# Reading the moving operand of every float32r product as two runs in turn

## The chip, the cores and the metric

The kernel runs on one core of a Trainium2 chip, as one program and one launch. The metric is the device time of that program in microseconds, taken as the median of several runs. TensorE (PE in the profile) does the products, VectorE (DVE), ScalarE (ACT) and GpSimd (POOL) do the elementwise work, and SyncE (SP) issues the DMAs.

## The reference

An attention over a window of 128 positions feeds two feed-forward layers. What is computed, cut to what matters:

```python
# 4 batches, 8 heads, 576 positions, 64 per head -> x is 2304 tokens x 512
x = attention(q, k, v)                  # window 128, bias -slope*|i-j|, softmax
h = x @ moe_w_in                        # first layer: 512 -> 2048
x = (relu(h) ** 2) @ moe_w_out          # 2048 -> 512
gate = 1 / (1 + exp(-(x @ w_gate)))     # second layer: 512 -> 1536, twice
val = x @ w_val
out = (gate * val) @ w_out              # 1536 -> 512
```

The inputs are float32; the weights reach the chip as 64-bit floats and are turned into 32-bit ones by a few bit operations.

## The kernel before

**Products in three parts.** Outside the attention every product is made of float32r matmuls. An operand is split into a high part (an ACT copy that rounds to float32r) and a low part (operand minus high part, on DVE or POOL), and high x high, high x low and low x high are added up in PSUM. So each product of 128 x 128 weights with 256 or 320 columns is three matmuls. Each matmul loads its own 128-column stationary operand (PEld in the profile) and then streams its moving operand of 256 or 320 columns past it.

**Stage A.** The attention and the first layer run chunk by chunk. There are eight chunks of tokens; the first four have 256 columns, the last four 320. For each of 16 slices of the hidden width, `h_step` makes h (lines 833 to 835, moving operand `x`), ACT takes Relu (847), DVE or ACT squares, an ACT copy through the helper at line 338 and a subtraction through the helper at line 335 write the two parts into the tile `gs` (850, 851), and `y_step` multiplies them with the output weights (870, moving operand `gs`). The products stand in the order H(f), Y(f-1), H(f+1), Y(f), so that a slice's elementwise work runs under the products of its neighbours. After the last slice `evac` copies the four y banks to SBUF, and they go to a scratch tensor in DRAM, 512 rows by tokens. The attention's own products and transposes are plain float32 and stand between these on TensorE.

**Weights of the second layer.** `prepare` turns them into 32 bits, splits them and their four Strassen sums into high and low parts (`split`, called by `pieces`), and `put` stores these in a scratch tensor. Each tile there holds high and low part of 256 columns side by side. `fetch` brings them back, one 256 KB tile at a time, for each block of tokens.

**Stage B.** The first block has 256 tokens (`xb` with n = 0, `gv`, `o_step`), and the other four have 512 each and go through Strassen's seven products (`xb`, `part`, `gv_strassen` at line 995, `o_strassen` at line 1168, `o_last` at line 1254). In the gate and value products the tokens are the moving operand; in the output products the weights are.

**What sets the order.** A planner (`Plan.schedule`) runs at build time. It gives each operation an engine, a place on it and a buffer, by priorities and assumed durations, and its list is written out as it stands. The change leaves those durations alone.

Of the kernel before, what the change touches and what calls it, by code (L numbers as in the profile page):

```python
# [287 lines left out]
def attention_moe_moe2_kernel(ctx: ExitStack, tc, q, k, v, w_in, w_out1, w_gate, w_val, w_out2, out):  # L288
# [54 lines left out]

    def chunk_steps(n):
        l = [("H", n, 0)]
        for f in range(1, F1):
            l += [("H", n, f), ("Y", n, f - 1)]
        return l + [("Y", n, F1 - 1)]
# [135 lines left out]
    def prepare(kind, f0, prio):  # L484
# [16 lines left out]
        as_halves = lambda p, z: p().rearrange("p k (z n) -> p z k n", z=2)[:, z]  # L501

        def pieces(t_, keys, k, prio):
            p = new("pp", [128, 2, 512], F32R)
            split(lambda: t_().rearrange("p (k n) -> p k n", k=2), lambda: as_halves(p, 0), lambda: as_halves(p, 1), keys, p, prio)
            put(u, p, k, prio + .1)
# [317 lines left out]
    def h_step(n, f, e0):  # L824
        N = width[n]
        w, x = W["in", f], X[n]
        ps = new("h", [128, 512], F32)
        xk = [(x, a, hp, p) for a in range(2) for hp in range(HP) for p in range(len(chunks[n]))]
        for half in range(2):
            def go(e, half=half):  # L830
                for cc in range(half * CC // 2, (half + 1) * CC // 2):
                    c = slice(cc * 128, cc * 128 + 128)
                    nc.tensor.matmul(ps()[:, :N], w[0]()[:, c], x()[:, 0, cc, :N], start=cc == 0, stop=False)  # L833
                    nc.tensor.matmul(ps()[:, :N], w[0]()[:, c], x()[:, 1, cc, :N], start=False, stop=False)  # L834
                    nc.tensor.matmul(ps()[:, :N], w[1]()[:, c], x()[:, 0, cc, :N], start=False, stop=cc == CC - 1)  # L835
# [13 lines left out]
        op({"ACT": act_ns(N)} if n >= 7 else {"DVE": dve_ns(N), "ACT": act_ns(N)}, square, r=[ps, g], w=[g], prio=ep)  # L849
        op({"ACT": act_ns(N)}, copy(lambda: gs()[:, 0, :N], lambda: g()[:, :N]), r=[g], w=[(gs, 0)], prio=ep)  # L850
        op(dve_or_pool(N), minus(lambda: gs()[:, 1, :N], lambda: g()[:, :N], lambda: gs()[:, 0, :N]),
           r=[g, (gs, 0)], w=[(gs, 1)], prio=ep, port=True)
        G[n, f] = gs
# [3 lines left out]
    def y_step(n, f, e0):  # L857
# [5 lines left out]
        for e_ in range(CC):  # L863
            y = Y[n][e_]

            def go(e, y=y, e_=e_):
                c = slice(e_ * 128, e_ * 128 + 128)
                for p, (a, b) in enumerate(((0, 0), (0, 1), (1, 0))):

                    nc.tensor.matmul(y()[:, c0:c0 + N], w[a]()[:, c], gs()[:, b, :N], start=f == 0 and p == 0 and n != 1,  # L870
# [4 lines left out]
        if f == F1 - 1:  # L875
            for e_ in range(CC):
# [3 lines left out]
                def evac(e, y=y, ys=ys):  # L880
                    if e == "ACT":
                        nc.scalar.activation(out=ys()[:, :N], in_=y()[:, c0:c0 + N], func=AF.Copy)
                    else:
                        nc.vector.tensor_copy(ys()[:, :N], y()[:, c0:c0 + N])
# [17 lines left out]
    def xb(n, prio):  # L902
        t0, NB = blocks[n]
        if n == 0:
            x = new("x", [128, 2, CC, NMAX], F32R)
            for c0 in range(0, CC, 2):
                ysg = new("ysg", [128, 512], F32)
                src = lambda ysg=ysg: ysg().rearrange("p (c t) -> p c t", c=2)
                part = lambda z, c0=c0: x()[:, z, c0:c0 + 2, :NB]
# [4 lines left out]
                op({"ACT": act_ns(512)}, copy(lambda part=part: part(0), src), r=[ysg], w=[(x, 0, c0)], prio=prio)  # L914
                op(dve_or_pool(512), minus(lambda part=part: part(1), src, lambda part=part: part(0)),
# [26 lines left out]
        def part(name, src, pr):  # L942
            (bh, ih), (bl, il) = where[name]
            op({"ACT": act_ns(512)}, copy(lambda: bh()[:, ih], flat(src)), r=[src], w=[(bh, ih)], prio=pr)
            op({"DVE": dve_ns(512)}, minus(lambda: bl()[:, il], flat(src), lambda: bh()[:, ih]), r=[src, (bh, ih)], w=[(bl, il)], prio=pr, port=True)
# [31 lines left out]
    def gv_strassen(n, kind, f, e0):  # L977
# [9 lines left out]
        def product(name, ps, start=False):  # L987
# [102 lines left out]
    def gv(n, f, e0):  # L1090
# [3 lines left out]
        for z, kind in enumerate(("gate", "val")):  # L1094
# [6 lines left out]
            def go(e, ps=ps, part=part):  # L1101
                for cc in range(CC):
                    nc.tensor.matmul(ps()[:, :NB], part(0, cc), x(0, cc), start=cc == 0, stop=False)
                    nc.tensor.matmul(ps()[:, :NB], part(0, cc), x(1, cc), start=False, stop=False)  # L1104
                    nc.tensor.matmul(ps()[:, :NB], part(1, cc), x(0, cc), start=False, stop=cc == CC - 1)
# [14 lines left out]
    def o_step(n, f, e0):  # L1120
# [4 lines left out]
        for t in range(NB // 128):  # L1125
            o = O[n][t]

            def go(e, t=t, o=o):
                c = slice(t * 128, t * 128 + 128)
                for k in range(2):  # L1130
                    for i, (a_, z) in enumerate(((ah, 0), (ah, 1), (al, 0))):
                        nc.tensor.matmul(o()[:, k * 256:k * 256 + 256], a_()[:, c], w[k]()[:, z * 256:z * 256 + 256],  # L1132
# [20 lines left out]
    def o_strassen(n, f, part, e0, last=False):  # L1153
# [82 lines left out]
    def o_last(n, f, part, e0):  # L1236
# [8 lines left out]
        for z, (i, j, ps, sum_, fresh) in enumerate(todo):  # L1245
            fine = (i, j) == (0, 1)
            for t in range(2):
                for part_ in range(2):
# [3 lines left out]
                    def go(e, t=t, part_=part_, hi=hi, lo=lo, ch=ch, wt=wt, ps=ps, fresh=fresh):  # L1252
                        for k, (a_, y) in enumerate(((hi, 0), (hi, 1), (lo, 0))):
                            nc.tensor.matmul(ps()[:, 256 * t:256 * t + 256], a_()[:, ch + 128 * t:ch + 128 * t + 128], wt()[:, 256 * y:256 * y + 256],
# [122 lines left out]
```

## Time and profile before

| | us |
|---|---|
| median of 3 runs | 959.66 (958.83 to 960.71) |
| span of the profiled execution, first to last instruction | 955.4 |
| TensorE busy, of that span | 941.8 |
| TensorE loading weights | 908.9 |
| VectorE busy | 630.4 |
| ScalarE busy | 559.8 |
| GpSimd busy | 186.4 |

The span is one execution under the profiler; the runs were timed without it. The 4.3 us between the span and the median lie outside the first and the last instruction. Busy times of the engines overlap. A matmul's duration in the trace includes the time in which its result drains, so the matmuls of a stream overlap each other; what one costs in a stream is read from start to start.

### The profile page before, as it was taken

The numbers are of one execution on the slowest core, as the hardware profiler recorded it, in microseconds if no ns is written. First come the engines' busy times: TensorE is split into PE (matmuls) and PEld (weight loads), VectorE is DVE, ScalarE is ACT, GpSimd is POOL, SyncE is SP. The second block draws the span as 40 slices with busy tenths as digits, with TensorE's granted clock in tenths as the row PEclk, the third lists the DMA queues.
The fourth block names the chain that finished last, engine by engine and source line by source line (L and its number), as shares of the span: only waits on it lengthen the run. The fifth ranks groups of instructions, "written<-read, shape, count | busy, mean of one in ns | idle before, by whom it ended". The sixth has DMA issues, their size and how long they took to land.

```text
span 955.4 us, 21188 instructions
## 1 busy us (share of the span) xinstructions
PE 941.8 (99%) x7656; PEld 908.9 (95%) x7656; DVE 630.4 (66%) x1621; ACT 559.8 (59%) x1496; POOL 186.4 (20%) x270
## 2 busy tenths in 40 slices
PE   8899999999999999999999999999999999999998
PEld 6689999999999999999999999999999999999998
DVE  7999988677676676767753234555855585476555
ACT  6987876777676586667554523544544544454442
POOL 3611111313132121123000010102312230122000
PEclk9999999999999999999999999999999999999999
DMA  9755547584665766665699791666877787678931
GB/s 230 178 166 169 170 128 227 203 228 154 188 182 175 215 191 173 193 187 177 223 300 385 286 322 43 210 212 211 264 236 219 226 268 223 212 240 277 331 100 45
DMA packets 181448, 199.83 MB, mean 209 GB/s; under 512 B 80097, under 2 KB 113377, under 8 KB 181345
## 3 DMA queue, kind: packets, MB, share of 16 engines
q1 hardware_dynamic: 181344, 198.48, 67.1%
q8 instruction: 61, 1.00, 0.5%
q14 instruction: 43, 0.34, 0.1%
HBM read 151.26 MB, written 47.19 MB: 208 GB/s over the span
## 4 chain that ended last, share of the span: by engine, by line
PE 94%; DVE 3%; ACT 1%; DMA 1%; SPq 1%; issue 0%; DVEq 0%
PE y L870 22%; PE pa L995 14%; PE pd L995 11%; PE o L1168 10%; PE h L833 7%; PE h L834 7%; PE h L835 7%; PE tv L806 3%; PE ts L679 2%; PE o L1132 2%; PE pd L1168 2%; PE tp L761 1%; DMA nq<-in_q_dram 1%; ACT st L711 1%; PE ts L670 1%; PE pv L1104 1%
## 5 line engine op out<-in xcount | busy, mean ns | idle before, releaser
L870 PE MATMUL y<-gs,wh 128*128 128x256 f32 (+1 forms) x1024 | 214.3, 301 | 1.3 <-DVE gs L335 1.3
L870 PEld LDWEIGHTS y<-gs,wh 128*128 128x128 f32 x1024 | 163.4, 189 | 8.5 <-issue 3.8
L833 PE MATMUL h<-x,wh 128*128 128x256 f32 (+1 forms) x512 | 154.2, 301 | 0.0
L834 PE MATMUL h<-x,wh 128*128 128x256 f32 (+1 forms) x512 | 151.3, 295 | 0.5 <-DVE x L335 0.5
L870 PE MATMUL y<-gs,wl 128*128 128x256 f32 (+1 forms) x512 | 151.4, 296 | 0.3 <-DVE wl L335 0.3
L835 PE MATMUL h<-x,wl 128*128 128x256 f32 (+1 forms) x512 | 151.2, 295 | 0.0
L338 ACT ACTIVATE cg<-pa 128x256 f32<-128x256 f32 x144 | 54.7, 382 | 109.6 <-PE pa L995 106.2
L847 ACT ACTIVATE r<-h 128x256 f32<-128x256 f32 (+1 forms) x128 | 51.9, 407 | 86.9 <-PE h L835 86.7
L335 DVE TENSOR_TENSOR gs<-r,gs 128x256 fp32r<-128x256 f32 (+1 forms) x122 | 58.0, 476 | 64.7 <-ACT gs L338 64.4
L833 PEld LDWEIGHTS h<-x,wh 128*128 128x128 f32 x512 | 96.7, 189 | 2.6 <-issue 1.0
L834 PEld LDWEIGHTS h<-x,wh 128*128 128x128 f32 x512 | 96.8, 189 | 0.7 <-DVE x L335 0.7
L870 PEld LDWEIGHTS y<-gs,wl 128*128 128x128 f32 x512 | 96.6, 189 | 0.5 <-DVE wl L335 0.5
L835 PEld LDWEIGHTS h<-x,wl 128*128 128x128 f32 x512 | 96.5, 189 | 0.0
L771 POOL TENSOR_SCALAR_AFFINE_SELECT pt<-pt 128x256 f32<-128x256 f32 (+1 forms) x120 | 61.5, 539 | 135.3 <-ACT pt L765 134.3
L995 PE MATMUL pa<-x,st 128*128 128x256 f32 x576 | 84.3, 282 | 0.0
L1011 DVE TENSOR_TENSOR cg<-cg,pd 128x256 f32<-128x256 f32 x96 | 40.4, 421 | 61.6 <-PE pd L995 60.3
L995 PEld LDWEIGHTS pa<-x,st 128*128 128x128 f32 x576 | 75.2, 189 | 0.0
L1168 PE MATMUL o<-wr,ah 128*128 128x256 f32 x414 | 68.0, 281 | 0.0
L711 ACT ACTIVATE st<-st,sm 128x128 f32<-128x128 f32 x144 | 56.6, 402 | 16.9 <-DVE sm L704 16.7
L1168 PE MATMUL o<-so,ah 128*128 128x256 f32 x414 | 64.0, 281 | 0.0
L338 ACT ACTIVATE gs<-r 128x256 fp32r<-128x256 f32 (+1 forms) x128 | 56.5, 442 | 6.2 <-PE y L870 3.3
L1168 PEld LDWEIGHTS o<-wr,ah 128*128 128x128 f32 x414 | 57.3, 189 | 0.0
(197 smaller groups left out, 2044.5 us busy)
## 6 DMA issues: line engine op xcount, KB each, us to landing
st<-wscr SPq DMA_DIRECT2D x192, 256.0 KB, 3.6
wscr<-pp SPq DMA_DIRECT2D x72, 512.0 KB, 3.4
so<-wscr SPq DMA_DIRECT2D x93, 256.0 KB, 4.1
raw<-in_moe_w_out_dram SPq DMA_DIRECT2D x28, 512.0 KB, 3.8
wr<-wscr SPq DMA_DIRECT2D x54, 256.0 KB, 5.3
raw<-in_moe_w_in_dram SPq DMA_DIRECT2D x16, 512.0 KB, 4.3
vs<-in_v_dram SPq DMA_DIRECT2D x24, 256.0 KB, 5.5
raw<-in_moe_w_gate_dram SPq DMA_DIRECT2D x12, 512.0 KB, 3.9
```

The costliest lines, as they stand in the source:

```text
L335: return lambda e: eng(e).tensor_tensor(out=out(), in0=a(), in1=b(), op=ALU.subtract)
L338: return lambda e: nc.scalar.activation(out=out(), in_=in_(), func=AF.Copy, scale=scale)
L711: op({"ACT": 386}, lambda e, x=x: nc.scalar.activation(out=st()[:, x, :], in_=st()[:, x, :], func=AF.Exp, bias=sm()[:, x:x + 1], scale=-1. ...
L771: op({"POOL": pool_sel(512 // nq)}, lambda e: nc.gpsimd.affine_select(out=pt_of(what, j), in_=pt_of("own", j), pattern=[[0, 512 // (nq * c ...
L833: nc.tensor.matmul(ps()[:, :N], w[0]()[:, c], x()[:, 0, cc, :N], start=cc == 0, stop=False)
L834: nc.tensor.matmul(ps()[:, :N], w[0]()[:, c], x()[:, 1, cc, :N], start=False, stop=False)
L835: nc.tensor.matmul(ps()[:, :N], w[1]()[:, c], x()[:, 0, cc, :N], start=False, stop=cc == CC - 1)
L847: op({"ACT": act_ns(N, True)}, lambda e: nc.scalar.activation(out=g()[:, :N], in_=ps()[:, :N], func=AF.Relu), r=[ps], w=[g], prio=ep, also ...
L870: nc.tensor.matmul(y()[:, c0:c0 + N], w[a]()[:, c], gs()[:, b, :N], start=f == 0 and p == 0 and n != 1, stop=f == F1 - 1 and p == 2, skip_ ...
L995: nc.tensor.matmul(ps()[:, :256], w()[:, z * 256 + cc * 128:z * 256 + cc * 128 + 128], x, start=start and cc == 0 and i == 0, stop=cc == 1 ...
L1011: op({"DVE": dve_ns(256)} if psum else dve_or_pool(256), lambda e: eng(e).tensor_tensor(out=quarter(i, j)(), in0=quarter(i, j)(), in1=src( ...
L1168: nc.tensor.matmul(o()[:, 256 * t:256 * t + 256], a_()[:, c_ + 128 * t:c_ + 128 * t + 128], w()[:, 256 * z:256 * z + 256], start=start and ...
```

## The change

A new helper, `in_turn`, takes a run of N columns as two halves of N/2 and reads them in turn: column 0 of the first half, column 0 of the second, column 1 of the first, and so on. In the built program the moving operand of a 256-column product was one run of 256 elements and is now 128 pairs, the two elements of a pair lying 128 elements (512 bytes) apart; with 320 columns they lie 160 elements apart. All 6,534 float32r products of the computation get this pattern: 4,998 of 256 columns and 1,536 of 320. The attention's float32 products, the transposes and the 50 spin products at the start keep theirs.

So that results come out in place, the order in which operands lie is changed where they are split. In the first layer `x` lies as before, so that h comes out with its columns in turn; the splits into `gs` read every second column of it (`from_turns`) and write two runs (`runs`), which puts the columns back in order, and the evacuation of y does the same. In the second layer the splits read every second element of the source and write the two halves of a run, so that reading in turn gives the original order. That holds for the weights of the output product (`pieces`), for the first block (`xb`) and for the Strassen operands (`part`).

No instruction is added or removed. Apart from line numbers, the rows of instructions on each of the five engines, with their buffers, are the same word for word before and after; only access patterns differ.

```diff
+    def in_turn(x):
+        return x.rearrange("p (i c) -> p c i", i=2)
+
+    def runs(x):
+        return x.rearrange("p (i c) -> p i c", i=2)
+
+    def from_turns(x):
+        return x.rearrange("p (c i) -> p i c", i=2)
...
-        as_halves = lambda p, z: p().rearrange("p k (z n) -> p z k n", z=2)[:, z]
+        if kind == "out2":
+            as_halves = lambda p, z: p().rearrange("p k (z i n) -> p z k i n", z=2, i=2)[:, z]
+            as_read = lambda t_: t_().rearrange("p (k n i) -> p k i n", k=2, i=2)
+        else:
+            as_halves = lambda p, z: p().rearrange("p k (z n) -> p z k n", z=2)[:, z]
+            as_read = lambda t_: t_().rearrange("p (k n) -> p k n", k=2)
...
-            split(lambda: t_().rearrange("p (k n) -> p k n", k=2), lambda: as_halves(p, 0), lambda: as_halves(p, 1), keys, p, prio)
+            split(lambda: as_read(t_), lambda: as_halves(p, 0), lambda: as_halves(p, 1), keys, p, prio)
...
-                    nc.tensor.matmul(ps()[:, :N], w[0]()[:, c], x()[:, 0, cc, :N], start=cc == 0, stop=False)
+                    nc.tensor.matmul(ps()[:, :N], w[0]()[:, c], in_turn(x()[:, 0, cc, :N]), start=cc == 0, stop=False)
...
-        op({"ACT": act_ns(N)}, copy(lambda: gs()[:, 0, :N], lambda: g()[:, :N]), r=[g], w=[(gs, 0)], prio=ep)
-        op(dve_or_pool(N), minus(lambda: gs()[:, 1, :N], lambda: g()[:, :N], lambda: gs()[:, 0, :N]),
+        op({"ACT": act_ns(N)}, copy(lambda: runs(gs()[:, 0, :N]), lambda: from_turns(g()[:, :N])), r=[g], w=[(gs, 0)], prio=ep)
+        op(dve_or_pool(N), minus(lambda: runs(gs()[:, 1, :N]), lambda: from_turns(g()[:, :N]), lambda: runs(gs()[:, 0, :N])),
...
-                    nc.tensor.matmul(y()[:, c0:c0 + N], w[a]()[:, c], gs()[:, b, :N], start=f == 0 and p == 0 and n != 1,
+                    nc.tensor.matmul(y()[:, c0:c0 + N], w[a]()[:, c], in_turn(gs()[:, b, :N]), start=f == 0 and p == 0 and n != 1,
...
-                        nc.scalar.activation(out=ys()[:, :N], in_=y()[:, c0:c0 + N], func=AF.Copy)
+                        nc.scalar.activation(out=runs(ys()[:, :N]), in_=from_turns(y()[:, c0:c0 + N]), func=AF.Copy)
                     else:
-                        nc.vector.tensor_copy(ys()[:, :N], y()[:, c0:c0 + N])
+                        nc.vector.tensor_copy(runs(ys()[:, :N]), from_turns(y()[:, c0:c0 + N]))
...
-            op({"ACT": act_ns(512)}, copy(lambda: bh()[:, ih], flat(src)), r=[src], w=[(bh, ih)], prio=pr)
-            op({"DVE": dve_ns(512)}, minus(lambda: bl()[:, il], flat(src), lambda: bh()[:, ih]), r=[src, (bh, ih)], w=[(bl, il)], prio=pr, port=True)
+            turns = lambda: src().rearrange("p c (t i) -> p c i t", i=2)
+            hi, lo = ((lambda b=b, k=k: b()[:, k].rearrange("p (c i t) -> p c i t", c=2, i=2)) for b, k in ((bh, ih), (bl, il)))
+            op({"ACT": act_ns(512)}, copy(hi, turns), r=[src], w=[(bh, ih)], prio=pr)
+            op({"DVE": dve_ns(512)}, minus(lo, turns, hi), r=[src, (bh, ih)], w=[(bl, il)], prio=pr, port=True)
...
-                        nc.tensor.matmul(ps()[:, :256], w()[:, z * 256 + cc * 128:z * 256 + cc * 128 + 128], x,
+                        nc.tensor.matmul(ps()[:, :256], w()[:, z * 256 + cc * 128:z * 256 + cc * 128 + 128], in_turn(x),
...
-                nc.tensor.matmul(o()[:, 256 * t:256 * t + 256], a_()[:, c_ + 128 * t:c_ + 128 * t + 128], w()[:, 256 * z:256 * z + 256],
+                nc.tensor.matmul(o()[:, 256 * t:256 * t + 256], a_()[:, c_ + 128 * t:c_ + 128 * t + 128], in_turn(w()[:, 256 * z:256 * z + 256]),
```

Left out are the same edits of the other matmul calls (lines 834, 835, 1103 to 1105, 1132, 1254) and of the split in `xb` for the first block.

## Rows read from the trace of the kernel before

**Rows 1.** The page: busy us (share of the span) and instructions of each engine

```profile
PE 941.8 (99%) x7656; PEld 908.9 (95%) x7656; DVE 630.4 (66%) x1621; ACT 559.8 (59%) x1496; POOL 186.4 (20%) x270
```

**Rows 2.** The page: the chain that ended last, share of the span by engine

```profile
PE 94%; DVE 3%; ACT 1%; DMA 1%; SPq 1%; issue 0%; DVEq 0%
```

**Rows 3.** TensorE's waits, longest and shortest: us in total, times, longest

```profile
PE warm L1332 <- DVE identr L382: 1.8, 1, 1.8
...
PE pa L995 <- DVE cg L1040: 0.2, 1, 0.2
```

**Rows 4.** Windows: us; each engine's busy us (instructions); PEclk granted; DMA share, GB/s

```profile
100.00:200.00 100.00, 100.00 (x852) 95.76 (x852) 82.69 (x205) 71.40 (x189) 18.00 (x28) 1.00 0.60 188
...
700.00:800.00 100.00, 100.00 (x845) 100.00 (x844) 60.80 (x122) 47.56 (x111) 20.83 (x18) 1.00 0.76 236
```

**Rows 5.** Groups on PE by shape: busy us, mean ns of one

```profile
L870 PE MATMUL y<-gs,wh 128*128 128x320 f32 x512 | 117.4, 316 | 0.0
L870 PE MATMUL y<-gs,wh 128*128 128x256 f32 x512 | 96.9, 286 | 1.3 <-DVE gs L335 1.3
...
L1254 PE MATMUL pa<-so,ah 128*128 128x256 f32 x6 | 1.0, 279 | 0.0
```

**Rows 6.** Timeline of PE in stage B: start us, us until the last has drained

```profile
699.74 0.88 PE L995 MATMUL pa<-x,st 128*128 128x256 f32 x6
700.46 0.88 PE L995 MATMUL pd<-x,st 128*128 128x256 f32 x6
701.18 0.51 PE L1168 MATMUL o<-so,ah 128*128 128x256 f32 x3
701.53 0.88 PE L995 MATMUL pa<-xp,wr 128*128 128x256 f32 x6
```

**Rows 7.** Timeline of PE late in stage A, 320 columns

```profile
506.00 0.31 PE L833 MATMUL h<-x,wh 128*128 128x320 f32 x1
...
507.76 0.46 PE L870 MATMUL y<-gs,wh 128*128 128x320 f32 x2
...
511.28 0.46 PE L870 MATMUL y<-gs,wh 128*128 128x320 f32 x2
```

**Rows 8.** Timeline of PE: float32 transposes of 128 columns, one group behind another

```profile
22.55 0.60 PE L580 MATMUL tk<-identr,nk 128*128 128x128 f32 x4
22.98 0.60 PE L761 MATMUL tp<-identr,st 128*128 128x128 f32 x4
```

**Rows 9.** Timeline of PE: the first products of the program (float32r spin products)

```profile
1.78 4.40 PE L1332 MATMUL warm<-identr 128*128 128x256 f32 x21 [1.78 <-DVE identr L382]
6.13 0.66 PE L580 MATMUL tq<-identr,nq 128*128 128x128 f32 x4
```

**Rows 10.** Groups on ACT: a read of every second word, and a contiguous one

```profile
L338 ACT ACTIVATE pp<-tw 128x512 fp32r<-128x512 f32 x36 | 22.5, 624 | 4.1 <-DVE tw L471 1.7 <-DMA wscr<-pp 1.5 <-DVE tg L471 0.6
...
L461 ACT ACTIVATE tw<-raw 128x512 f32<-128x512 f32 x18 | 12.0, 669 | 0.1
```

**Rows 11.** Groups on DVE: a contiguous subtraction, and one source of every second word

```profile
L335 DVE TENSOR_TENSOR pp<-tw,pp 128x512 fp32r<-128x512 f32 x33 | 24.0, 726 | 11.2 <-ACT pp L338 10.5
...
L471 DVE SCALAR_TENSOR_TENSOR tw<-raw,tw 128x512 int32<-128x512 int32 x18 | 13.0, 724 | 0.2
```

**Rows 12.** A group on POOL: a contiguous subtraction

```profile
L335 POOL TENSOR_TENSOR pp<-tg,pp 128x512 fp32r<-128x512 f32 x6 | 7.7, 1288 | 39.5 <-DVE ts L692 19.0 <-DVE gs L335 11.5 <-ACT pp L338 8.1
```

**Rows 13.** Evacuations of y, on ACT and on DVE

```profile
L882 ACT ACTIVATE yz<-y 128x320 f32<-128x320 f32 x8 | 3.5, 438 | 4.3 <-PE y L870 3.2 <-PE h L834 1.1
...
L884 DVE COPY yz<-y 128x320 f32<-128x320 f32 x8 | 3.8, 490 | 2.5 <-PE h L834 1.7 <-PE h L835 0.7 <-PE y L870 0.2
```

**Rows 14.** Timeline of ACT and of DVE around rows 7: the splits of one slice

```profile
507.96 0.44 ACT L847 ACTIVATE r<-h 128x320 f32<-128x320 f32 x1 [2.07 <-PE h L835]
...
509.44 0.49 DVE L335 TENSOR_TENSOR gs<-r,gs 128x320 fp32r<-128x320 f32 x1 [3.02 <-ACT gs L338]
```

More of the change, by code (lines that the diff above doesn't have):

```diff
@@ L832, in go @@
                     c = slice(cc * 128, cc * 128 + 128)
-                    nc.tensor.matmul(ps()[:, :N], w[0]()[:, c], x()[:, 0, cc, :N], start=cc == 0, stop=False)
-                    nc.tensor.matmul(ps()[:, :N], w[0]()[:, c], x()[:, 1, cc, :N], start=False, stop=False)
-                    nc.tensor.matmul(ps()[:, :N], w[1]()[:, c], x()[:, 0, cc, :N], start=False, stop=cc == CC - 1)
+                    nc.tensor.matmul(ps()[:, :N], w[0]()[:, c], in_turn(x()[:, 0, cc, :N]), start=cc == 0, stop=False)
+                    nc.tensor.matmul(ps()[:, :N], w[0]()[:, c], in_turn(x()[:, 1, cc, :N]), start=False, stop=False)
+                    nc.tensor.matmul(ps()[:, :N], w[1]()[:, c], in_turn(x()[:, 0, cc, :N]), start=False, stop=cc == CC - 1)
             op({"PE": 3 * CC // 2 * pe_ns(N)}, go, r=xk + list(w), w=[ps] + ([("late",)] if n == NC - 1 and f == F1 - 2 else []), prio=e0 + half * .1)
@@ L908, in xb @@
                 src = lambda ysg=ysg: ysg().rearrange("p (c t) -> p c t", c=2)
-                part = lambda z, c0=c0: x()[:, z, c0:c0 + 2, :NB]
+                turns = lambda ysg=ysg: ysg().rearrange("p (c t i) -> p c i t", c=2, i=2)
+                part = lambda z, c0=c0: x()[:, z, c0:c0 + 2, :NB].rearrange("p c (i t) -> p c i t", i=2)
                 op({"SP": 475}, lambda e, c0=c0, src=src: nc.sync.dma_start(
@@ L913, in xb @@
                    prio=prio - 6, data=728, also=[x])
-                op({"ACT": act_ns(512)}, copy(lambda part=part: part(0), src), r=[ysg], w=[(x, 0, c0)], prio=prio)
-                op(dve_or_pool(512), minus(lambda part=part: part(1), src, lambda part=part: part(0)),
+                op({"ACT": act_ns(512)}, copy(lambda part=part: part(0), turns), r=[ysg], w=[(x, 0, c0)], prio=prio)
+                op(dve_or_pool(512), minus(lambda part=part: part(1), turns, lambda part=part: part(0)),
                    r=[ysg, (x, 0, c0)], w=[(x, 1, c0)], prio=prio)
@@ L1102, in go @@
                 for cc in range(CC):
-                    nc.tensor.matmul(ps()[:, :NB], part(0, cc), x(0, cc), start=cc == 0, stop=False)
-                    nc.tensor.matmul(ps()[:, :NB], part(0, cc), x(1, cc), start=False, stop=False)
-                    nc.tensor.matmul(ps()[:, :NB], part(1, cc), x(0, cc), start=False, stop=cc == CC - 1)
+                    nc.tensor.matmul(ps()[:, :NB], part(0, cc), in_turn(x(0, cc)), start=cc == 0, stop=False)
+                    nc.tensor.matmul(ps()[:, :NB], part(0, cc), in_turn(x(1, cc)), start=False, stop=False)
+                    nc.tensor.matmul(ps()[:, :NB], part(1, cc), in_turn(x(0, cc)), start=False, stop=cc == CC - 1)
             op({"PE": 3 * CC * pe_ns(NB)}, go, r=xkeys + w + [("late",)], w=[ps], prio=e0 + z)
@@ L1131, in go @@
                     for i, (a_, z) in enumerate(((ah, 0), (ah, 1), (al, 0))):
-                        nc.tensor.matmul(o()[:, k * 256:k * 256 + 256], a_()[:, c], w[k]()[:, z * 256:z * 256 + 256],
+                        nc.tensor.matmul(o()[:, k * 256:k * 256 + 256], a_()[:, c], in_turn(w[k]()[:, z * 256:z * 256 + 256]),
                                          start=f == 0 and k == 0 and i == 0, stop=f == F2 - 1 and i == 2, skip_group_check=True)
@@ L1253, in go @@
                         for k, (a_, y) in enumerate(((hi, 0), (hi, 1), (lo, 0))):
-                            nc.tensor.matmul(ps()[:, 256 * t:256 * t + 256], a_()[:, ch + 128 * t:ch + 128 * t + 128], wt()[:, 256 * y:256 * y + 256],
+                            nc.tensor.matmul(ps()[:, 256 * t:256 * t + 256], a_()[:, ch + 128 * t:ch + 128 * t + 128], in_turn(wt()[:, 256 * y:256 * y + 256]),
                                              start=fresh and t == 0 and part_ == 0 and k == 0, stop=part_ == 1 and k == 2, skip_group_check=True)
```

## The prediction

> **What bounds the kernel now.** I read the page first. TensorE is busy for 941.8 of 955.4 us [rows 1], and the chain that ended last runs through it for 94% of the span [rows 2]. Its list of waits has eleven rows, of which the longest is 1.8 us and the shortest 0.2 [rows 3]; all eleven add up to about 10 us, nearly all of it before 50 us. In the windows it is busy 100.00 of 100 us in the dense part of stage A and in stage B [rows 4]. So the end is set by the rate at which matmuls follow each other, and by little else.
>
> That rate is read from the timeline, start to start. In stage B, 15 products of 256 columns take 701.53 - 699.74 = 1.79 us, 119.3 ns each [rows 6], and the window from 700 to 800 us has 845 of them, 118.3 ns each [rows 4]. Late in stage A twelve of 320 columns take 507.76 - 506.00 = 1.76 us, 146.7 ns each [rows 7]. The granted clock is 1.00 there [rows 4], the upper of the two levels, 2.4 GHz, at which 256 columns stream in 106.7 ns and 320 in 133.3 ns. So each product costs 11.6 to 12.6 ns and 13.4 ns more than its columns. I call this the surplus. Two things are to be seen in it:
> - It hardly grows with the columns (12 against 13 ns), so it comes once per matmul, and each matmul has one load of 128 weight columns running beneath the stream of the one before.
> - It is gone where the moving operand is read at half the rate. Four float32 transposes of 128 columns, each with its own load, take 22.98 - 22.55 = 0.43 us, 108 ns each [rows 8], which is 0.83 ns per column; 128 columns at 1.2 GHz are 106.7 ns. The 21 spin products at the start take 6.13 - 1.78 = 4.35 us, 207 ns each [rows 9], where 256 columns at 1.2 GHz would be 213.
>
> So the load alone doesn't make the surplus. It appears when the moving operand is read at full rate while weights are read. That points to the reading of operands from SBUF, and the order of that reading is all that the change alters on TensorE.
>
> **The change part by part.** No instruction moves, so no queue is passed and no wait is added.
>
> *The products.* 6,534 get the new pattern. The list by shape has 33 rows of 256 columns, with 4,998 instructions, and five of 320 columns, with 1,536 (the first of each and the last stand in [rows 5]). The trace of before has no float32r product that hops, so I bound the new cost from both sides. Below: the surplus goes, and what stays is what the transposes keep, 108 - 106.7, about 2 ns with the rounding of the timeline [rows 8]. That saves 10 ns of 118.3 and 11 ns of 146.7: 4,998 x 10 = 50 us and 1,536 x 11 = 17 us, together 67 us. Above: each hop costs a read, and the moving operand comes at one column per cycle of the lower level [rows 9]: 207 ns for 256 columns and 207 x 320 / 256 = 259 ns for 320. That adds 4,998 x 89 = 445 us and 1,536 x 112 = 172 us, 617 us in all. I take the lower end. The transposes differ from the stream in type and shape as well, but the spin products are the same float32r product [rows 9], and in both the surplus is gone with the reading rate. So the surplus sits in the reading, and the reading is what is changed. That it changes for the better is an inference; no row shows it.
>
> *The splits.* They now read every second word. On ACT such a read of 512 took 669 ns where a contiguous one took 624 [rows 10], 45 ns more. About 102 splits of 512 columns and 128 of 256 or 320 (some 25 ns each by the same ratio) make 102 x 45 + 128 x 25 = 8 us on an engine that is busy for 559.8 of 955.4 us [rows 1]. On DVE an operation with one source of every second word took 724 ns, a contiguous subtraction 726 [rows 11], so nothing. POOL has no such row. A contiguous split there takes 1,288 ns [rows 12]; between nothing and a doubling I take nothing, as DVE shows. All this is hidden: a slice's h ends at 507.76, its splits end at 509.44 + 0.49 = 509.93, and its y products start at 511.28 [rows 7, 14], 1.35 us later. An added 25 ns disappears in that. Without this cover each of the 128 slices would pay it, 3 us.
>
> *The evacuations.* They read every second word of PSUM, for which there is no row: 32 of some 440 to 490 ns [rows 13], shared by ACT and DVE, two each per chunk. Between nothing and a doubling (0.9 us at each of seven changes of chunk, 6 us) I take nothing, because two slices of h stand between the last y of one chunk and the first of the next.
>
> *What is late next.* If products get faster, the work beside them must keep up. From 100 to 200 us DVE is busy for 82.7 of 100 us and ACT for 71.4 [rows 4]; were all 852 instructions there products of 256 columns, they would give up 8.5 us, and DVE would stand at 82.7 / 91.5 = 90%. Late in stage A the path from one slice to its use shortens by 24 x 11 = 0.26 us, and the 1.35 us of slack becomes 1.1. In stage B DVE is at 61% and the DMA engines at 0.76 [rows 4], which would become 66% and 0.83. So nothing takes over as the bound, but the planner's order has tight places in stage A. I let 6 us come back as new waits. At worst stage A, with 1,536 products of either width (15 + 17 us), gains nothing.
>
> *The sum.* 955.4 - 67 + 6 = 894 us of span. The median stands 4.3 us above the profiled span, so I predict **899 us**. With stage A gaining nothing it is 955.4 - 35 + 4.3 = 925; with no give-back 893; with two thirds of the surplus removed, 955.4 - 45 + 6 + 4.3 = 921. Its own range is 890 to 935.
>
> [...]
>
> **The rivals.**
>
> *The hop costs* (the other side). Neighbouring columns of the stream now lie 512 or 640 bytes apart, so a read may bring one column where it brought several, and TensorE can't be fed at 256 columns in 118.3 ns. For it: nothing in the trace reads a float32r moving operand in any order but straight through, and the transposes and spin products show what half the rate looks like. Against it: each of the two runs is still read in order, so whoever reads two runs side by side needs no more from memory than before. It decides from the point where a 256-column product takes more than 118.3 ns. In full it gives 955.4 + 617 + 4.3 = 1,577 us; a twentieth of its price gives 955.4 + 31 + 4.3 = 991.
>
> *The order of reading doesn't matter.* The surplus belongs to the hand-over from one set of weights to the next and is paid at full rate whatever the order. For it: it is the same for 256 and 320 columns, as a fixed hand-over would be. Against it: the transposes hand over weights too and keep only 2 ns. Then only the splits and evacuations count: 959.7 plus 0 to 6 us, 960 to 966. This is also the case in which the change doesn't do what it says, though the built program does carry the 128 pairs.
>
> *Something else takes over.* Products get faster, but the slices of stage A wait for DVE: 925 us as above. This is inside the forecast's own range.
>
> **How the numbers follow.** A measurement of this kernel can tell some 0.2%, 2 us, from no change. I give the forecast, with the third rival in it, 0.67; the order not mattering 0.13; the hop costing 0.20, of which a quarter pays so little that it stays below 990 us. The second splits about evenly between within 0.2% and slower by more. So faster 0.67, same 0.07, slower 0.26. The range must leave out no more than 2 in 10: from 890 it has to pass the second rival's 966 and the mild form of the first, so it ends at 990; left out are the full price of the hop (0.15) and a little below 890. The forecast's own range, 890 to 935, holds some 0.6 of the chance.
>
> **What would show it.** In the timeline of after, six products of 256 columns in stage B should start 0.65 us apart instead of 0.72, and twelve of 320 columns 1.63 instead of 1.76; the window from 700 to 800 us should hold some 920 products. The weight loads should follow in step. ACT's splits of 512 columns should read about 670 ns, DVE's stay near 726. TensorE's waits may grow from 10 to about 16 us, and those added should name DVE or ACT in stage A. The prediction is wrong in its main step if six products still take 0.72 us (the hand-over) or more (the hop), and wrong in its give-back if they are faster but the windows show TensorE below 97% anywhere between 60 and 900 us.

## The result and the profile after

The change takes the kernel from 959.5 to 916.9 us (913.7 to 918.6 in four runs). The ratio is 0.955, with a 95% interval of 0.953 to 0.958: 43 us, or 4.5%, faster. The forecast was 899 us. The profiled execution has a span of 911.5 us and is the quickest of the four; each of them lists a span 2.1 to 2.2 us below its time. The later executions of the kernel before, whose spans are listed too, show the same 2.1 to 2.2 us. So the 4.3 us that the prediction adds to the span lie only half outside the first and the last instruction. By that the profiled execution of the kernel before took some 957.6 us and was quicker than the median, as the one after is.

The page of the kernel after, busy us and share of the span by engine, and further down the shares of the chain that ended last [rows 1, 2]:

```profile
span 911.5 us, 21194 instructions
...
PE 895.3 (98%) x7656; PEld 861.4 (94%) x7656; DVE 632.4 (69%) x1621; ACT 574.2 (63%) x1496; POOL 194.2 (21%) x270
...
PE 86%; DVE 5%; ACT 4%; DMA 2%; POOL 1%; issue 1%; SPq 1%; ACTq 0%; DVEq 0%
```

TensorE is still the bound, but everything else now has 14% of the chain instead of 6%. Its windows in both stages, in the columns of [rows 4]:

```profile
100.00:200.00 100.00, 98.31 (x877) 93.54 (x875) 86.71 (x210) 79.50 (x194) 19.20 (x28) 1.00 0.64 195
...
700.00:800.00 100.00, 99.41 (x884) 98.83 (x883) 62.47 (x125) 49.83 (x114) 23.03 (x19) 1.00 0.76 243
```

From 700 to 800 us 884 products pass where 845 did, and TensorE is no longer busy all the time. The rate itself is in the timeline of PE, start us and us until the last has drained, first in stage B, then late in stage A [rows 6, 7]:

```profile
600.12 0.83 PE L1013 MATMUL pa<-x,wr 128*128 128x256 f32 x6
600.79 0.83 PE L1013 MATMUL pd<-xp,st 128*128 128x256 f32 x6
601.46 0.50 PE L1186 MATMUL o<-so,ah 128*128 128x256 f32 x3
```

```profile
479.96 0.30 PE L848 MATMUL h<-x,wh 128*128 128x320 f32 x1
...
481.59 0.43 PE L885 MATMUL y<-gs,wh 128*128 128x320 f32 x2
```

Six products of 256 columns take 0.67 us, 111.7 ns each, where they took 118.3 to 119.3. Twelve of 320 columns take 1.63 us, 135.8 ns each instead of 146.7.

What came back is seen in the waits and perhaps in the clock. The list of TensorE's waits (total us, times, longest) has grown from eleven rows and 10.5 us to twelve and 12.9 us, and now begins with another row [rows 3]:

```profile
PE y L885 <- DVE gs L335: 3.3, 4, 1.3
...
PE pd L1013 <- ACT qc L338: 0.6, 1, 0.6
```

One such place in stage A, in the timeline of PE: y has done one product of a group when it has to wait for the low part in `gs`.

```profile
111.98 0.28 PE L850 MATMUL h<-x,wl 128*128 128x256 f32 x1
112.09 0.28 PE L885 MATMUL y<-gs,wh 128*128 128x256 f32 x1
113.42 0.38 PE L885 MATMUL y<-gs,wh 128*128 128x256 f32 x1 [1.05 <-DVE gs L335]
```

In one stretch the clock was lower. Behind 6.50 us in which TensorE was busy for 5.10, the windows give the granted clock as 0.52, and from 52.00 to 54.50 us alone as 0.50:

```profile
45.00:51.50 6.50, 5.10 (x44) 3.76 (x46) 6.25 (x27) 4.76 (x17) 3.43 (x5) 1.00 0.36 109
51.50:55.00 3.50, 3.50 (x23) 2.99 (x20) 3.43 (x19) 3.50 (x15) 0.86 (x1) 0.52 0.56 138
```

In that stretch products of 256 columns start 213 ns apart, where 111.7 is usual. Some 3.4 us at half the clock (an estimate from the 0.52 over 3.50 us) cost at most 1.7 us. That the change brought it on is not shown. In the same windows of the kernel before, TensorE was busy for only 4.83 of 6.50 us and the clock stayed at 1.00. Other executions of the kernel before list a mean granted clock between 0.996 and 1.000, where this one lists 0.998.

### The profile page after: what moved, and what is told of

The parts are those of the page before. It is cut to its first block, busy times and chain, and to the rows that moved or that the text cites. A ratio compares the mean times of both kernels' runs of the same rounds, so it can differ in the third digit from the quotient of the medians.

```text
span 911.5 us, 21194 instructions
## 1 busy us (share of the span) xinstructions
PE 895.3 (98%) x7656; PEld 861.4 (94%) x7656; DVE 632.4 (69%) x1621; ACT 574.2 (63%) x1496; POOL 194.2 (21%) x270
## 4 chain that ended last, share of the span: by engine, by line
PE 86%; DVE 5%; ACT 4%; DMA 2%; POOL 1%; issue 1%; SPq 1%; ACTq 0%; DVEq 0%
PE y L885 19%; PE pa L1013 14%; PE pd L1013 11%; PE o L1186 10%; PE h L848 6%; PE h L849 6%; PE h L850 6%; PE tv L821 3%; PE ts L694 2%; PE o L1150 2%; PE pd L1186 2%; PE tp L776 1%; ACT st L726 1%; DVE wt L442 1%; POOL pt L786 1%; DVE wt L445 1%
## 5 line engine op out<-in xcount | busy, mean ns | idle before, releaser
L885 PE MATMUL y<-gs,wh 128*128 128x256 f32 (+1 forms) x1024 | 202.5, 293 | 3.3 <-DVE gs L335 3.3
L885 PEld LDWEIGHTS y<-gs,wh 128*128 128x128 f32 x1024 | 160.4, 190 | 11.2 <-DVE gs L335 4.2
L848 PE MATMUL h<-x,wh 128*128 128x256 f32 (+1 forms) x512 | 150.5, 294 | 0.5 <-DVE r L860 0.3
L849 PE MATMUL h<-x,wh 128*128 128x256 f32 (+1 forms) x512 | 147.2, 288 | 0.0
L850 PE MATMUL h<-x,wl 128*128 128x256 f32 (+1 forms) x512 | 147.1, 287 | 0.0
L885 PE MATMUL y<-gs,wl 128*128 128x256 f32 (+1 forms) x512 | 146.9, 287 | 0.0
L786 POOL TENSOR_SCALAR_AFFINE_SELECT pt<-pt 128x256 f32<-128x256 f32 (+1 forms) x120 | 66.9, 583 | 127.9 <-ACT pt L780 120.6
L1013 PE MATMUL pa<-x,st 128*128 128x256 f32 x576 | 80.4, 276 | 0.0
L1013 PEld LDWEIGHTS pa<-x,st 128*128 128x128 f32 x576 | 72.0, 192 | 0.0
L338 ACT ACTIVATE gs<-r 128x256 fp32r<-128x256 f32 (+1 forms) x128 | 63.5, 497 | 3.0 <-DVE r L860 0.4
L1186 PE MATMUL o<-so,ah 128*128 128x256 f32 x414 | 61.2, 275 | 0.0
```

What stands on the lines that cost most here:

```text
L338: return lambda e: nc.scalar.activation(out=out(), in_=in_(), func=AF.Copy, scale=scale)
L786: op({"POOL": pool_sel(512 // nq)}, lambda e: nc.gpsimd.affine_select(out=pt_of(what, j), in_=pt_of("own", j), pattern=[[0, 512 // (nq * c ...
L848: nc.tensor.matmul(ps()[:, :N], w[0]()[:, c], in_turn(x()[:, 0, cc, :N]), start=cc == 0, stop=False)
L849: nc.tensor.matmul(ps()[:, :N], w[0]()[:, c], in_turn(x()[:, 1, cc, :N]), start=False, stop=False)
L850: nc.tensor.matmul(ps()[:, :N], w[1]()[:, c], in_turn(x()[:, 0, cc, :N]), start=False, stop=cc == CC - 1)
L885: nc.tensor.matmul(y()[:, c0:c0 + N], w[a]()[:, c], in_turn(gs()[:, b, :N]), start=f == 0 and p == 0 and n != 1, stop=f == F1 - 1 and p == ...
```

## The experiments

**The reading by itself.** Streams of 60 float32r products were put behind the last store of the changed kernel, where nothing else runs: from 938 to 1068 us the windows show no work on DVE, ACT and POOL, a DMA share of 0.00 and a granted clock of 1.00. It is one execution, and all operands are ones. `m(n)` is a run of n words, `w` 128 weight columns, and `turn(x, i)` reads i runs in turn.

```diff
...
+        for _ in R: T(ps[:, :256], w, m(256), start=True, stop=True)
+        for _ in R: T(ps[:, :256], w, turn(m(256), 2), start=True, stop=True)
+        for _ in R: T(ps[:, :320], w, m(320), start=True, stop=True)
+        for _ in R: T(ps[:, :320], w, turn(m(320), 2), start=True, stop=True)
...
+        for _ in R: T(ps[:64, :256], w[:, :64], m(256), start=True, stop=True)
+        for _ in R: T(ps[:64, :256], w[:, :64], turn(m(256), 2), start=True, stop=True)
+        for _ in R: T(ps[:, :256], w, turn(m(256), 4), start=True, stop=True)
+        for _ in R: T(ps[:, :256], w, turn(m(256), 16), start=True, stop=True)
+        for _ in R: T(ps[:, :256], w, m(512).rearrange("p (c i) -> p i c", i=2)[:, 0], start=True, stop=True)
...
```

> The kernel after, with 14 streams of 60 products each put behind its last store, on a quiet chip: all float32r, one PSUM bank, constant data, each product with its own weight load. Two theories of the surplus, and both take 118 to 120 ns for 256 columns read straight and 111.7 in turn, 146.7 and 135.7 for 320 columns, 226 to 228 and 215.7 for 512. Theory one: the straight read at full rate collides with the reading of the 128 weight columns, so the surplus of some 12 ns is paid per weight load. [...] Theory two: the straight read is slow in itself and the weights have no part in it. Then 64 weight columns change nothing: 118 to 120 straight, 111.7 in turn. The other orders (four runs, sixteen runs, every second word, pairs of neighbours from two runs, runs 4 KB apart) show what of the pattern does it: if any hop will do, all give 111.7; if it takes two words that are not neighbours but stay within two runs, sixteen runs are slow, 200 ns or more; every second word tells whether hopping is needed at all. Weights read at every second word: 111.7 if the weight read has no such surplus.

The timeline of PE in that kernel; a row is one stream, and a 60th of the distance to the next row's start is what one product costs:

```profile
938.13 7.36 PE L1362 MATMUL bp<-bd 128*128 128x256 f32 x60
945.33 6.86 PE L1363 MATMUL bp<-bd 128*128 128x256 f32 x60
952.03 8.97 PE L1364 MATMUL bp<-bd 128*128 128x320 f32 x60
960.84 8.31 PE L1365 MATMUL bp<-bd 128*128 128x320 f32 x60
968.98 13.78 PE L1366 MATMUL bp<-bd 128*128 128x512 f32 x60
982.60 13.11 PE L1367 MATMUL bp<-bd 128*128 128x512 f32 x60
995.55 6.97 PE L1368 MATMUL bp<-bd 128*64 128x256 f32 x60
1002.36 6.71 PE L1369 MATMUL bp<-bd 128*64 128x256 f32 x60
1008.91 8.40 PE L1370 MATMUL bp<-bd 128*128 128x256 f32 x60
1017.15 13.36 PE L1371 MATMUL bp<-bd 128*128 128x256 f32 x60
1030.33 13.79 PE L1372 MATMUL bp<-bd 128*128 128x256 f32 x60
1043.93 10.19 PE L1373 MATMUL bp<-bd 128*128 128x256 f32 x60
1053.94 6.88 PE L1374 MATMUL bp<-bd 128*128 128x256 f32 x60
1060.65 7.35 PE L1375 MATMUL bp<-bd 128*128 128x256 f32 x60
```

| line | moving operand, weight columns | ns each |
|---|---|---|
| 1362, 1363 | 256 straight, in turn; 128 | 120.0, 111.7 |
| 1364, 1365 | 320 straight, in turn; 128 | 146.8, 135.7 |
| 1366, 1367 | 512 straight, in turn; 128 | 227.0, 215.8 |
| 1368, 1369 | 256 straight, in turn; 64 | 113.5, 109.2 |
| 1370, 1371 | four, sixteen runs in turn; 128 | 137.3, 219.7 |
| 1372 | every second word; 128 | 226.7 |
| 1373 | two neighbours from each run in turn; 128 | 166.8 |
| 1374 | two runs 4 KB apart; 128 | 111.8 |
| 1375 | 256 in turn; weights at every second word | 119.8 |

The last is (7.35 - 0.28) / 59, its 60 products less the last one's 283 ns until it has drained. Theory one holds in its main point: with 64 weight columns the straight read costs 113.5 instead of 120.0 ns, while the moving operand is the same. So of the 10.8 ns by which the straight read stands above the 109.2 of the read in turn with 64 weight columns, 6.5 go with half the weight columns and 4.3 stay. That the straight read costs nothing by itself is not shown, since no stream was run without a weight load. The streams with fewer weight columns also write fewer partitions of the result, and that was not varied alone. A second sign that the reading of the weights matters is the last stream: weights at every second word cost 119.8 ns with the moving operand in turn.

The 192 columns by which 512 exceed 320 add 80.2 ns read straight and 80.1 in turn, 0.417 to 0.418 ns each, or 2.4 columns per ns at a granted clock of 1.00. At that rate 256, 320 and 512 columns take 106.7, 133.3 and 213.3 ns (an estimate from these streams); that is the columns' own time. Read in turn, 320 and 512 columns take 135.7 and 215.8 ns, 2.4 to 2.5 ns more than that, about what the prediction let stay. And it is not that any hop will do. Of the orders tried only two runs gain anything, and it makes no difference whether they lie 512 bytes or 4 KB apart (111.7 and 111.8 ns). Four runs already cost more than the straight read (137.3 ns against 120.0), and sixteen runs or every second word (219.7 and 226.7 ns) cost about twice the columns' time.

**What is left at 256 columns.** 111.7 ns is 2.5 ns more than with 64 weight columns.

```diff
...
+        for _ in R: T(ps[:, :272], w, turn(m(272), 2), start=True, stop=True)
+        for _ in R: T(ps[:, :288], w, turn(m(288), 2), start=True, stop=True)
+        for _ in R: T(ps[:, :192], w, turn(m(192), 2), start=True, stop=True)
+        for _ in R: T(ps[:96, :256], w[:, :96], turn(m(256), 2), start=True, stop=True)
+        for _ in R: T(ps[:32, :256], w[:, :32], m(256), start=True, stop=True)
+        for _ in R: T(ps[:, :256], w, m(258).rearrange("p (i c) -> p c i", i=2)[:, :128], start=True, stop=True)
...
```

> Again streams of 60 products behind the last store, now on what is left over 109 ns at 256 columns read in turn (111.7, against 109.2 with 64 weight columns). Theory one, a floor of the weight load: the next product can't start before 128 weight columns are in, 111.7 ns whatever the moving operand. Then 192 columns in turn take 111.7 too (if they run at the same rate at all), 272 columns 115.8, 288 columns 122.5, and 96 weight columns with 256 columns give 109.2. [...] 32 weight columns, read straight: the surplus per weight column gives 106.7 + 2.5 + a quarter of 11 = some 110 to 112 ns. Operands and weights starting at another word (2 words on): the same 111.7, or 120 if the start of a run matters.

The timeline of PE, as above:

```profile
943.72 6.86 PE L1363 MATMUL bp<-bd 128*128 128x256 f32 x60
950.42 7.12 PE L1364 MATMUL bp<-bd 128*128 128x272 f32 x60
957.38 7.51 PE L1365 MATMUL bp<-bd 128*128 128x288 f32 x60
964.73 6.83 PE L1366 MATMUL bp<-bd 128*128 128x192 f32 x60
971.40 6.72 PE L1367 MATMUL bp<-bd 128*96 128x256 f32 x60
977.95 6.97 PE L1368 MATMUL bp<-bd 128*32 128x256 f32 x60
984.76 6.86 PE L1369 MATMUL bp<-bd 128*128 128x256 f32 x60
991.46 6.86 PE L1370 MATMUL bp<-bd 128*128 128x256 f32 x60
998.16 6.86 PE L1371 MATMUL bp<-bd 128*128 128x256 f32 x60
1004.86 6.86 PE L1372 MATMUL bp<-bd 128*128 128x256 f32 x60
1011.56 6.86 PE L1373 MATMUL bp<-bd 128*128 128x256 f32 x60
```

From start to start, 192 columns take 111.2 ns, 256 take 111.7, 272 take 116.0 and 288 take 122.5; 256 columns with 96 weight columns take 109.2. So below some 262 columns (an estimate: there the columns' time and 2.5 ns reach 111.7) the spacing no longer falls with the columns. With 128 weight columns no product of these streams starts earlier than 111 to 112 ns after the last, and theory one holds. A second run that starts 1, 2 or 4 words further off (lines 1369 to 1371), or operands or weights 2 words further on (1372, 1373), changed nothing: each of these five streams took 6.86 us, as the one in line 1363 did. The float32 transposes [rows 8] load 128 weight columns too and stay below this floor with 108 ns; why was not tried. One number missed: 32 weight columns read straight cost 113.5 ns, as much as 64, not 110 to 112. So the surplus of the straight read falls with the weight columns (120.0, 113.5 and 113.5 ns with 128, 64 and 32), but not in proportion, and 4.3 ns of it did not go away with them.

**The splits without the reading.** `in_turn` returns its argument.

```diff
     def in_turn(x):
-        return x.rearrange("p (i c) -> p c i", i=2)
+        return x
```

> All splits and evacuations as in the change, but every product reads straight through (results come out in the wrong column order). Theory: only the reading order of the products gives time, so this is no faster than before; if the dearer splits are hidden it is 959 to 961 us, and if they are part of the give-back it is 962 to 966.

It took 958.7 us against 959.1, ratio 1.000 (0.999 to 1.001). All the splits and evacuations of the change together cost nothing that can be measured while products are slow, and without the new reading order nothing is gained.

**The reading without the splits.** `runs` and `from_turns` return their argument, and the splits of the second layer are those of before.

> Every product reads in turn, as in the change, but all splits and evacuations read straight as before (results come out in the wrong column order). The dearer splits alone cost nothing where products were slow. Theory: the give-back of some 8 us comes from products catching up with VectorE and ScalarE, and the dearer splits (some 14 us more on ScalarE) have a part in it: 911 to 914 us, against 914 to 919 with them. If the splits have no part: 914 to 919.

915.3 us, ratio 0.954 (0.953 to 0.956), against 0.955 (0.953 to 0.958) for the whole change: no difference that these runs can tell. The dearer splits have no measurable part in the give-back, so the first of the two expectations falls.

**Each stage alone.** Products and splits of one stage as in the change, those of the other as before. One of the edits, from the run that changes stage A alone:

```diff
-                        nc.tensor.matmul(ps()[:, :256], w()[:, z * 256 + cc * 128:z * 256 + cc * 128 + 128], in_turn(x),
+                        nc.tensor.matmul(ps()[:, :256], w()[:, z * 256 + cc * 128:z * 256 + cc * 128 + 128], straight(x),
```

> Only the products and splits of stage A (first layer) are changed; the second layer is as before. 1,536 products of 256 columns at 7.1 ns and 1,536 of 320 at 10.9 ns are 27.7 us; if the give-back of 8 us lies mostly in stage A, the gain is some 21 us, 938 to 940 us. If stage A waited for VectorE and gained little, 950 us or more.

> Only the products and splits of the second layer are changed. 3,462 products at 7.1 ns are 24.6 us; with a give-back of 2 to 3 us the gain is some 22 us, 937 to 939 us. The two halves together should then give the 43 us of the whole change. If the give-back came from stage B, 945 us.

Stage A alone took 936.3 us, 22.8 us less than 959.1 (ratio 0.977, 0.975 to 0.978), and stage B alone 937.6, 21.5 us less (0.978, 0.977 to 0.979). Together that is 44.3 us, and the whole change gives 42.6. So each stage keeps its own gain, and neither hides the other's. Stage A did some 2 us better than expected, stage B came out as expected. Without any give-back they would have gained 27.7 and 24.6 us, so some 5 us of it lie in stage A and 3 in stage B.

**Can the give-back be planned away?** The planner places work by assumed durations of a product. It was told others, everything else as in the change. The edit for 111.7 ns:

```diff
-    return 2.45 + n / 2.4
+    return max(111.7, 2.5 + n / 2.4) if n >= 256 else 2.45 + n / 2.4
```

> The change, with the planner told what the trace of it shows: 111.7 ns for 256 columns (it assumed 109.1), 72 and 37 ns more for the splits into gs, 160 ns more for those of the second layer. The order of work shifts with that. Theory: the give-back of 8 us is work that comes late in an order that was planned with other durations; with the right ones up to half of it comes back, 911 to 915 us. Rival: the waits are chance collisions that any order has, and the time stays at 914 to 919 us, or a few us on either side of it.

> The change, with the planner told only the measured 111.7 ns for products of 256 columns (it assumes 109.1) and nothing of the splits. The replan with both told lost 11 us. If the dearer splits in the plan did that, this one stays at 914 to 919 us; if any new order does it, since the old one had been found good by trying, this one too is slower, 920 us or more. If it is 911 or less, the right durations do help and the splits were told too dear.

> The change, with the planner told the durations of before, 119.7 ns for 256 and 146.3 ns for 320 columns, so that its order leaves other engines more time than they have. If the waits that came with the change are a matter of a plan too tight, the looser plan has more of them, 920 us or more; if any new order is worse, 920 to 930 as well; if the order hardly matters, 914 to 919.

> The change, with the planner assuming 106.7 ns for 256 and 133.3 ns for 320 columns, faster than the products are (111.7 and 135.8). Assumed 109.1, 111.7 and 119.7 gave 917, 927 and 948 us. If what counts is that the plan leaves room, an assumption below the true time goes on in that direction: 908 to 915 us. If the order in hand is a lucky one and any other is worse, 920 us or more.

> The same with 102.4 and 128 ns assumed. By room in the plan 905 to 915 us, with less left to gain (the products alone need some 905); by the lucky order 920 or more. If 106.7 helps and this one is worse again, the best assumption lies between.

| assumed for 256 columns, ns | us | ratio (95%) |
|---|---|---|
| 102.4 | 921.2 | 0.960 (0.958 to 0.962) |
| 106.7 | 929.3 | 0.970 (0.968 to 0.972) |
| 109.1 (the change) | 916.9 | 0.955 (0.953 to 0.958) |
| 111.7 | 927.2 | 0.968 (0.967 to 0.969) |
| 111.7, splits dearer | 927.9 | 0.968 (0.966 to 0.969) |
| 119.7 | 947.8 | 0.989 (0.988 to 0.990) |

A plan that believes in slow products is clearly worse: at 119.7 ns some 31 of the 43 us are lost. Otherwise there is no trend. The true durations give a worse order than those assumed in the change, with the splits (927.9 us, where 911 to 915 were expected, or 914 to 919 by the rival) and without them. Durations below the true ones don't help either: 106.7 ns is worse than 102.4. All five orders stand at 920 us or more, as was expected if any new order is worse than the one in hand. TensorE's longest waits under the slowest plan (us in total, times, longest) are spread over both stages:

```profile
PE h L848 <- DVE r L860: 3.4, 2, 2.0
PE y L885 <- DVE gs L335: 3.1, 6, 1.0
PE o L1150 <- ACT asp L338: 3.0, 1, 3.0
```

So the order in hand is the best of the six, and the time of an order varies by 10 us and more with the durations assumed. That a better order exists is not excluded.

## Why the prediction was right or wrong

The direction, the cause and the place were right. The gain was 43 us where 61 were forecast, and most of the difference is in one term.

- **What bounds the kernel:** right. Products alone, at a new spacing, make the gain, in both stages alike.
- **The columns' own time:** the 106.7 and 133.3 ns that the prediction takes off at 2.4 GHz stand in no row of before. The runs bear them out: the streams add 0.417 to 0.418 ns a column, and at a granted clock of 0.50 the kernel after starts products of 256 columns 213 ns apart, twice 106.7.
- **The surplus is a matter of reading while weights are read:** right in the main. That the order of reading removes it was, as the prediction says, an inference without a row; now it is shown: at 320 columns 13.4 ns became 2.5, with nothing else changed in the streams. That the weight load has a part in it is borne out as well: the straight read gets cheaper with 64 weight columns (113.5 instead of 120.0 ns), though these also write half the partitions, and weights at every second word cost 119.8 ns in turn instead of 111.7. That it is all a matter of the weight load is not shown: 4.3 ns stay with 64 and with 32 weight columns. What was said for it from the spin products proves little. The 207 ns [rows 9] are a mean over products of different pace. By the starts in the trace the first takes 380 ns, the next fifteen some 213 each, and the four behind them 117 to 163. 213 ns is also what the kernel after takes for 256 columns read in turn at a granted clock of 0.50, and its transposes of 128 columns start 213 ns apart there too, instead of 108. So in those fifteen the whole of TensorE may have been slower, and not the reading alone. That is an inference: the windows give 1.00 there, though the trace's record of the clock begins only at 5.45 us, about where the pace changes.
- **The term of 320 columns:** 11 ns were taken, 10.9 measured (146.7 to 135.8), 17 us.
- **The term of 256 columns:** this is the step that failed. The transposes' row was taken as what is left when the surplus goes, so 118.3 was to become 108 ns, 10 ns saved and 50 us. It became 111.7, so 4,998 products gave 7 ns each (118.7 on average before, by the starts of all of them), 35 us. The transposes showed that a weight load need not cost more than 2 ns over 106.7 when the operand beside it is read at half the rate (128 columns in 108 ns). They could not show that in a float32r stream at full rate with 128 weight columns the next product starts no earlier than some 111 ns after the last, as the stream of 192 columns shows with its 111.2 ns. That is 15 of the 18 us. Products of 320 columns are above that floor, so their term came out.
- **The give-back:** 6 us taken, a guess from tight places that had no row for its size, so that it came near is partly luck. By the profiled executions 955.4 - 35 - 17 = 903 against 911.5, so 8 us. Added up over the trace, the gaps between starts that exceed the usual spacing by more than 14 ns hold 23.3 us in excess of it, where they held 17.1; the attention's matmuls take 2 us more. Together that is the 8 us; the stretch at the lower clock is in it with at most 1.7. The waits are in stage A on `gs`, as said, and a few in stage B on copies out of PSUM, which the prediction did not have. By the medians the give-back is some 9 us (916.9 against 959.5 - 52 = 907.5), since the profiled execution was the quickest. The dearer splits have no measurable part in it; what makes the waits otherwise is not shown. The clock was not in the forecast.
- **The splits:** hidden, as said, but their prices and their number were wrong. ACT's splits of 512 columns into `x` took 786 ns, not 670 (rows below). Those into `pp` took 655 ns, but that is a mean of two kinds: only the 24 of the output product's weights read every second word, not all 72 as the prediction counts, and by an estimate they took some 717 (the other two thirds at 624, as in the run with the splits of before). The splits into `gs` got 72 ns dearer at 256 columns (415 to 487) and 37 at 320 (470 to 507), not 25. In all ACT was busy for 14 us more (574.2 against 559.8), not 8. DVE's splits into `pp` stayed at 728 ns and POOL's at 1,284 [rows 11, 12], means of both kinds too; DVE's into `x` went from 801 to 821. The evacuations stayed at 437 and 487 ns, against 438 and 490 before [rows 13]: every second word of PSUM cost nothing there.
- **The hop costs:** wrong for two runs, right for any other pattern tried. Two runs in turn took 111.7 ns, less than the 120.0 of the straight read; two neighbours from each run took 166.8, four runs 137.3, sixteen 219.7 and every second word 226.7.
- **The order doesn't matter:** fell with the first two streams (120.0 and 111.7 ns).
- **Something else takes over:** fell. Stage A alone gained 22.8 us, where this rival gave it nothing.
- **What would show it:** twelve products of 320 columns were to take 1.63 us and took 1.63; six of 256 columns 0.65, and took 0.67; the window was to hold 920 products and holds 884. Whether the sign against the give-back appeared depends on the length of the windows, which the prediction left open. In windows of 100 us from 100 us on TensorE never fell below 98%. In windows of 20 us it stood at 96% from 80 to 100 us (19.17 us busy) and at 93% from 100 to 120 (18.64), both in stage A, where the forecast had put the new waits.

## What to carry to other kernels

Read what a matmul costs from start to start and take the columns' own time off it. What is left has to be explained, and if it doesn't grow with the columns (here it was 13.3 to 13.7 ns at 256, 320 and 512), look at the weight load, which had a part in it here. In these float32r streams, each product with its load of 128 weight columns, two runs read in turn were worth 7 to 8 ns at 256 columns and 11 ns at 320 and 512, as long as the operand can be laid out so in a step that is hidden anyway. A floor has to be looked for on the other side of a cost before the whole of it is counted as gain. Here products of 272 columns or more would have got all of it, by an estimate: in turn they take 116.0 ns, 2.7 above their columns' time, but no straight stream of that width was run.

## What the runs showed of the hardware

Beside products read in turn, ACT was slower where it reads every second word: 755 ns instead of 670. The groups on ACT (busy us, mean ns of one) first with all splits changed and the products straight, then with the products in turn and the splits of before, then with both:

```profile
L435 ACT ACTIVATE wt<-raw 128x512 f32<-128x512 f32 x32 | 21.3, 670 | 8.6 <-DMA raw<-in_moe_w_in_dram 6.3 <-DMA raw<-in_moe_w_out_dram 2.1
...
L338 ACT ACTIVATE x<-xf 128x512 fp32r<-128x512 f32 x20 | 12.7, 681 | 3.6 <-PE pd L1013 1.2 <-DVE xf L335 1.2 <-PE pv L1123 1.1
```

```profile
L435 ACT ACTIVATE wt<-raw 128x512 f32<-128x512 f32 x32 | 24.0, 755 | 12.4 <-DMA raw<-in_moe_w_in_dram 9.5 <-DMA raw<-in_moe_w_out_dram 2.6
...
L338 ACT ACTIVATE x<-xf 128x512 fp32r<-128x512 f32 x20 | 11.7, 624 | 4.3 <-DVE xf L335 2.4 <-PE pv L1123 1.0 <-PE pd L1013 0.9
```

```profile
L435 ACT ACTIVATE wt<-raw 128x512 f32<-128x512 f32 x32 | 24.0, 754 | 9.2 <-DMA raw<-in_moe_w_in_dram 7.3 <-DMA raw<-in_moe_w_out_dram 1.8
...
L338 ACT ACTIVATE pp<-tw 128x512 fp32r<-128x512 f32 x36 | 23.6, 655 | 6.4 <-DMA wscr<-pp 4.4 <-DVE tg L481 1.0 <-DVE tw L481 0.9
...
L338 ACT ACTIVATE x<-xf 128x512 fp32r<-128x512 f32 x20 | 14.8, 786 | 4.1 <-DVE xf L335 2.2 <-PE pv L1123 1.0 <-PE pd L1013 1.0
```

The read of `raw`, every second word in all three, takes 670 ns beside straight products and 755 beside products in turn, though nothing of it was changed. With stage A alone in turn, where `raw` is read for `wt`, it takes 758 ns, and with stage B alone 672. The pace of the kernel as a whole is not the reason: under the slowest plan (947.8 us) it still takes 759. The split into `x` takes 624 ns when it reads straight beside products in turn, and 627 in the kernel before. It takes 681 when it reads every second word beside straight products, and 786 when both are changed. DVE shows it on the same source, to a smaller extent: its two operations that read `raw` for `wt` take 718 and 691 ns beside straight products, 752 and 728 beside products in turn. So in these rows the order in which TensorE reads changes what a read costs on ACT, by 85 ns, and on DVE, by 34 to 37.

The surcharge differs with the width of the products beside it. The weights of the second layer are read while the chunks of 256 columns run (first row, from 140 to 260 us) and while those of 320 run (second row, from 270 to 490), after the change:

```profile
L471 ACT ACTIVATE tw<-raw 128x512 f32<-128x512 f32 x7 | 5.4, 773 | 0.6 <-DMA raw<-in_moe_w_val_dram 0.5
```

```profile
L471 ACT ACTIVATE tw<-raw 128x512 f32<-128x512 f32 x11 | 7.5, 684 | 0.0
```

With straight products in both (the run of the splits without the reading) the same operation took 668 and 666 ns. So most of ACT's surcharge comes beside products of 256 columns, whose two runs lie 512 bytes apart, and little beside those of 320, with 640 bytes. That fits the 72 and 37 ns on the splits into `gs`. Whether the distance of the runs or the rate of the products does it was not tried. What makes two runs cheap and four dear was not tried further and stays open.
